# Reading w and u by other DMAs, and a new order for the first unit of an RWKV and SiLU kernel

## Chip, cores and metric

The kernel runs on one core of a Trainium2 chip. The metric is device time in microseconds (us), the median of several executions. A profile shows one execution: its span goes from the first to the last instruction, and the execution's own time is a little longer than its span.

## What is computed

A recurrent attention (RWKV-5 style) over 4 batches, 8 heads, 768 steps and head size 48, followed by a two-layer network with SiLU between its layers:

```python
# r, k, v: (4, 8, 768, 48); w, u: (8, 48)
for t in range(S):
    kt, vt, rt = k[:, :, t], v[:, :, t], r[:, :, t]
    cur = einsum('bhd,bhe->bhde', u[None] * kt, vt)
    y[:, :, t] = einsum('bhd,bhde->bhe', rt, state + cur)
    state = w[None, :, :, None] * state + einsum('bhd,bhe->bhde', kt, vt)
x = y.transpose(0, 2, 1, 3).reshape(B * S, H * D)      # (3072, 384)
h = x @ w_in                                           # w_in (384, 2048)
out = (h * sigmoid(h)) @ w_out                         # w_out (2048, 384)
```

## The kernel before

Time is cut into 6 chunks of 128 steps. A unit is one chunk of one batch; the 24 units run chunk by chunk, batch by batch, so units 0 to 3 are the first chunk of the four batches. Inside a unit the recurrence becomes matrix work: r is multiplied by powers of w, k by inverse powers of w (both with the head dimension on the partitions, two heads to a pair and four pairs to a unit), their product is masked to the strict lower triangle (`am`), and the masked scores times v give y. The term with u on the diagonal is a sum of r*k*u over the head dimension (`rku`), times v (`vu`), added to y.

All is issued by hand in one fixed order (`manual_schedule`); each engine takes its instructions in that order, and waits between engines follow from what tiles they share. Several queues matter here.

- SP issues the loads: r, k and v of a unit are three DMAs of 192 KB (`load`, L71), in 192-byte rows. The loads of units 0 to 3 go out at once; those of units 4 and 5 are held back by a small GpSimd memset (L464) that overlaps one of their destinations.
- VectorE makes the powers of w (`pif`, seven doubling products, L156), the decay products (`p1`, L226 for r, L230 for k), the masks (`am`, L276), the bonus sums (L197) and y (L300).
- GpSimd (POOL) makes k*u (`ku`, L180), r*k*u (`rku_f`, L186), v times the bonus (`vu`, L203), and k scaled for the state (`kc`, L191). It also asks for moe_w_in, which its DMAs turn into half precision on the way, in four parts of 512 columns (`win_part`, L417). Ahead of the first stands a one-column copy of r of unit 1 into `gate` (L434), so that it isn't asked for before that load has landed.
- TensorE transposes r and k, multiplies, and runs the first layer (`l1`, L358: one column tile of 128 is three matmuls) and the second (`l2`, L370) as fillers between the units' work. Junk matmuls (`spin`, L125) keep it busy at the start.

At the very start w and u are each read as four short rows (`wrow`, `urow`, L85: one DMA of 1.5 KB each). A TensorE transpose turns w into columns in PSUM (`to_cols`, L129), from which VectorE starts the powers. Five spins stand ahead of that transpose and four behind it. u goes through a transpose, an ACT copy (L134), four transposes of a broadcast column (`to_rows`, L147) and an ACT copy (L149) to become `u_bc`, u spread over all 128 partitions. This is called between the r and the k product of unit 0 (`mid`).

The order around unit 0 on GpSimd: gate, first part of moe_w_in, ku and rku_f of unit 0, ku and rku_f of unit 1, second part of moe_w_in, vu of unit 1, ku and rku_f of unit 2, kc of unit 0, third and fourth part, the memset at L464.

Of the kernel before, what the change touches and what calls it, by code (L numbers as in the profile page):

```python
# [8 lines left out]
FP = mybir.dt.float32  # L9
F16 = mybir.dt.float16  # L10
AF = mybir.ActivationFunctionType
ALU = mybir.AluOpType
# [3 lines left out]
def kernel(  # L16
# [11 lines left out]
    nc = tc.nc  # L28

    B, H, S, D = r.shape  # L30
    C = 128
    NCH = S // C
    HD = H * D
    NP = H // 2
    PW = 2 * D
    PR = 64 + D
# [7 lines left out]
    cst = ctx.enter_context(tc.tile_pool(name="cst", bufs=1))  # L44
    big = ctx.enter_context(tc.tile_pool(name="big", bufs=1))
    wrk = ctx.enter_context(tc.tile_pool(name="wrk", bufs=2))
    ps = ctx.enter_context(tc.tile_pool(name="ps", bufs=1, space=bass.MemoryType.PSUM))
# [3 lines left out]
    rin = [big.tile([128, H, 64], FP, name=f"rin{i}") for i in range(NIN)]  # L51
# [9 lines left out]
    def unit(i):  # L61
        return divmod(i, B)

    def load(i, mid=None):
        if i >= NU:
            return
        sc, b = unit(i)
        for t, src in ((rin, r), (kin, k), (vin, v)):
            if t is vin and mid:
                mid()  # L70
            nc.sync.dma_start(out=t[i % NIN][:, :, 0:D],  # L71
                              in_=src[b, :, sc * C:sc * C + C, :]
                              .rearrange("h t d -> t h d"))

    wrow = cst.tile([NP, 2, 64], FP)
    urow = cst.tile([NP, 2, 64], FP)
    junk = cst.tile([128, 512], F16)
    nc.vector.memset(junk, 0.0)  # L80
    for t in (wrow, urow):
        nc.vector.memset(t[:, :, D:64], 1.0)

    def load_row(t, src):
        nc.sync.dma_start(out=t[:, :, 0:D], in_=bass.AP(tensor=src.tensor, offset=0,  # L85
                                                        ap=[[PW, NP], [D, 2], [1, D]]))

    load_row(wrow, w)
    load(0, mid=lambda: load_row(urow, u))
    for i in range(1, B):  # L90
        load(i)
    for t in (rin, kin):
        nc.vector.memset(t[0][:, :, D:64], 0.0)
    ident = cst.tile([128, 128], FP)
# [5 lines left out]
        out=maskM, in_=maskM, compare_op=ALU.is_ge, fill=0.0,  # L100
# [17 lines left out]
    def spin(n, t=None):  # L118

        if t is None:  # L120
            t = ps.tile([128, 512], FP, name="spin", tag="t", bufs=5)
        else:
            t = t.rearrange("s p t -> s (p t)")
        for _ in range(n):
            nc.tensor.matmul(t, junk[:, 0:128], junk, start=True, stop=True)  # L125

    def to_cols(row, copy):
        t = ps.tile([128, 512], FP, name="cols", tag="t", bufs=5)
        nc.tensor.transpose(t[0:PR, 0:NP], row.rearrange("p j d -> p (j d)")[:, 0:PR],  # L129
                            ident[0:NP, 0:NP])  # L130
        if copy is None:
            return t[0:PR, 0:NP]
        c = cst.tile([PR, NP], FP, name="cols_sb")
        copy(out=c, in_=t[0:PR, 0:NP])  # L134
        return c

    spin(5)
    wT = to_cols(wrow, None)
    spin(4)
    u_bc = cst.tile([128, H, D], FP)  # L140
    lamC = cst.tile([128, H, D], FP)

    def to_rows(dst, cols):

        t = ps.tile([128, NP, 2, 64], FP, name="rows", tag="t", bufs=5)
        for p in range(NP):
            nc.tensor.transpose(t[:, p, :, :].rearrange("t j d -> t (j d)")[:, 0:PR],  # L147
                                cols(p), ident[0:PR, 0:PR])
        nc.scalar.copy(out=dst.rearrange("t (p j) d -> t p j d", j=2), in_=t[:, :, :, 0:D])  # L149


    nc.vector.tensor_copy(out=pi[:, 0:NP, 1:2], in_=wT.unsqueeze(2))
    nc.vector.reciprocal(out=pi[:, NP:2 * NP, 1:2], in_=wT.unsqueeze(2))
    n = 1
    while n < C:
        nc.vector.tensor_tensor(  # L156
            out=pi[:, :, 1 + n:1 + 2 * n], in0=pi[:, :, 1:1 + n],
            in1=pi[:, :, n:n + 1].broadcast_to([PR, 2 * NP, n]), op=ALU.mult)
        n *= 2
    lamR = pi[:, 0:NP, 0:C]  # L160
    lamK = pi[:, NP:2 * NP, 1:C + 1]
# [15 lines left out]
    def nat_ku(i):  # L177
        L = live.setdefault(i, {})
        L["ku"] = wrk.tile([128, H, D], FP, name="ku")
        nc.gpsimd.tensor_tensor(out=L["ku"], in0=kin[i % NIN][:, :, 0:D], in1=u_bc,  # L180
                                op=ALU.mult)

    def nat_rk(i):
        L = live[i]
        L["rku_f"] = wrk.tile([128, H, D], FP, name="rku_f")
        nc.gpsimd.tensor_tensor(out=L["rku_f"], in0=rin[i % NIN][:, :, 0:D], in1=L["ku"],  # L186
                                op=ALU.mult)
# [12 lines left out]
    def bonus_vu(i):  # L200
        L = live[i]
        L["vu"] = wrk.tile([128, H, D], FP, name="vu", bufs=3)
        nc.gpsimd.tensor_tensor(out=L["vu"], in0=vin[i % NIN],  # L203
                                in1=L["rku"].unsqueeze(2).broadcast_to([128, H, D]),
                                op=ALU.mult)
# [5 lines left out]
            nc.scalar.activation(out=L["vu"][:, h, :], in_=vin[i % NIN][:, h, :],  # L211
                                 func=AF.Copy, scale=L["rku"][:, h:h + 1])

    def p1(i, mid=None, spins=0):
        n = i % NIN
        L = live.setdefault(i, {})
        tr = ps.tile([128, NP, C], FP, name="tr", tag="t", bufs=5)
        tk = ps.tile([128, NP, C], FP, name="tk", tag="t", bufs=5)
        spin(spins, tr)
        for t, src in ((tr, rin), (tk, kin)):  # L220
            flat = src[n].rearrange("p h d -> p (h d)")
            for p in range(NP):
                nc.tensor.transpose(t[0:PR, p, :], flat[:, 128 * p:128 * p + PR], ident)  # L223
        rk = wrk.tile([PR, 2, NP, C], FP, name="rk")
        L["rT"] = rk[:, 0]
        nc.vector.tensor_tensor(out=L["rT"], in0=tr[0:PR], in1=lamR, op=ALU.mult)  # L226
        if mid:
            mid()
        L["kT"] = rk[:, 1]
        nc.vector.tensor_tensor(out=L["kT"], in0=tk[0:PR], in1=lamK, op=ALU.mult)  # L230

    def p1t(i):

        n = i % NIN
        L = live.setdefault(i, {})
        xs = [ps.tile([128, 2, NP, 64], FP, name="xs", tag="t", bufs=5) for _ in range(2)]
        for a, src in enumerate((rin, kin)):
            flat = src[n].rearrange("p h d -> p (h d)")
            for p in range(NP):
                for g in range(2):  # L240
                    t = slice(64 * g, 64 * g + 64)
                    nc.tensor.transpose(xs[g][0:PR, a, p, :],  # L242
                                        flat[t, 128 * p:128 * p + PR], ident[t, t])
        rk = wrk.tile([PR, 2, NP, C], FP, name="rk")
        L["rT"] = rk[:, 0]
        L["kT"] = rk[:, 1]
        L["xs"] = xs, rk
# [13 lines left out]
    def p2(i, spins=0, nxt=None, late=False):  # L261
        L = live[i]
        ae = ps.tile([128, NP, C], FP, name="ae", tag="t", bufs=5)
        ao = ps.tile([128, NP, C], FP, name="ao", tag="t", bufs=5)
        spin(spins, ae)
        for p in range(NP):
            nc.tensor.matmul(ae[:, p, :], L["kT"][0:D, p, :], L["rT"][0:D, p, :],  # L267
                             start=True, stop=True)
            nc.tensor.matmul(ao[:, p, :], L["kT"][64:PR, p, :], L["rT"][64:PR, p, :],  # L269
                             start=True, stop=True)  # L270
        if nxt is not None:
            p1t(nxt)
        L["am"] = []
        for a in (ae, ao):
            am = wrk.tile([128, NP, C], F16, name="am", bufs=4)
            nc.vector.tensor_tensor(out=am, in0=a,  # L276
                                    in1=maskM.unsqueeze(1).broadcast_to([128, NP, C]),
                                    op=ALU.mult)
            L["am"].append(am)
        if nxt is not None and not late:  # L280
            p1d(nxt)
# [124 lines left out]
            f()  # L406


    def to_cols_u():
        t = to_cols(urow, nc.scalar.copy)  # L410
        to_rows(u_bc, lambda p: t[:, p:p + 1].broadcast_to([PR, 128]))

    zero = junk[0:PR, 0:HD].rearrange("r (p c) -> r p c", p=NP)
    gate = cst.tile([128, 1], FP)

    def win_part(c0, c1):
        nc.gpsimd.dma_start(out=win[:, :, c0:c1],  # L417
                            in_=moe_w_in[:, c0:c1].rearrange("(q p) n -> p q n", p=128))
# [4 lines left out]
            in_=moe_w_out[1024 * g:1024 * g + 1024, :].rearrange("(f p) n -> p f n", p=128))  # L423


    p1(0, mid=to_cols_u)
    nat_v(0)
    lamCT = cst.tile([PR, NP, C], FP)
    for p in range(NP):
# [1 line left out]
                             scale=pi[:, p, C:C + 1])  # L431

    nc.scalar.copy(out=st[0], in_=zero)
    nc.gpsimd.tensor_copy(out=gate, in_=rin[1][:, 0, 0:1])  # L434
    win_part(0, 512)
    nat_ku(0)
    nat_rk(0)
    p2(0)
    p1(1, spins=1)
    bonus_sum(0)  # L440
    nat_ku(1)
# [3 lines left out]
    to_rows(lamC, lambda p: lamCT[:, p, :])  # L445
    bonus_act(0)
    nc.scalar.copy(out=st[1], in_=zero)
    win_part(512, 1024)
    bonus_sum(1)
    bonus_vu(1)  # L450
    p2(1, spins=2)
    p3e(0)
    spin(4)
# [2 lines left out]
    spin(1)  # L456
    p4(0)
    p1(2)
    nat_ku(2)
    nat_rk(2)  # L460
# [177 lines left out]
```

## Time and profile before

| what | value |
|---|---|
| median of 11 runs | 198.71 us (198.15 to 199.88) |
| the profiled execution's own time | 199.09 us |
| its span | 197.4 us |
| TensorE matmul busy | 189.8 us, 96% of the span |
| VectorE, ScalarE, GpSimd busy | 115.4, 91.1, 115.0 us |
| granted TensorE clock, of full speed | 0.999 |
| DMA, mean rate | 122 GB/s over the span; 167 to 209 GB/s from 5 to 55 us |
| one load of 192 KB, issue to landing | 3.5 to 3.8 us in the median |
| a part of moe_w_in, issue to landing | 6.1 us in the median |

How to read it: DVE is VectorE, ACT is ScalarE, POOL is GpSimd, PE is TensorE's matmuls and PEld its weight loads, which run ahead of and beside the matmuls. A row of the timeline gives the start, the duration, the engine, the source line, the operation with its output and inputs, and in brackets the idle time of the engine before it with what ended that. The share of busy time is a mean over the whole; TensorE's first 16 us are partly spins, and after some 25 us it is hardly ever idle.

### The profile page before, as it was taken

What the parts mean: (1) busy time and instruction counts of PE and PEld (TensorE: products, weight loads), DVE (VectorE), ACT (ScalarE), POOL (GpSimd) and SP (SyncE); (2) the same over time, 40 slices, a digit from 0 to 9 for tenths busy, and PEclk for the clock granted to TensorE, in tenths of its full rate; (3) what the DMA queues carried; (4) which work ended last, traced back from release to release, by engine and by line L of the source; (5) the groups of instructions that cost most, each with busy time, mean ns of one, the idle gap of its engine ahead of it and who ended that gap; (6) DMA issues with size and microseconds to landing.
All of it is one profiled execution on the core that took longest, in us unless ns stands there. A gap on an engine that the chain in (4) does not pass through costs nothing.

```text
span 197.4 us, 4920 instructions
## 1 busy us (share of the span) xinstructions
PE 189.8 (96%) x1919; PEld 127.4 (65%) x1919; DVE 115.4 (58%) x233; ACT 91.1 (46%) x207; POOL 115.0 (58%) x145
## 2 busy tenths in 40 slices
PE   7889999999999999999999999999999999999993
PEld 2747878787765976675566766557666546644563
DVE  6677658885857746975675686476576344210121
ACT  3475487799212652205861216682016680069300
POOL 4499959979975795697669647735437710000000
PEclk9999999999999999999999999999999999999999
DMA  4999999999898976757466387520321011210022
GB/s 82 209 186 167 186 203 179 184 189 202 165 196 176 221 173 149 173 136 160 89 122 140 100 182 160 105 58 0 106 60 43 20 22 43 78 61 0 3 81 80
DMA packets 89696, 24.12 MB, mean 122 GB/s; under 512 B 82888, under 2 KB 89672, under 8 KB 89672
## 3 DMA queue, kind: packets, MB, share of 16 engines
q1 hardware_dynamic: 85992, 20.66, 48.1%
q0 software_dynamic: 3680, 3.15, 10.9%
q8 instruction: 15, 0.25, 0.5%
q14 instruction: 9, 0.07, 0.1%
HBM read 20.45 MB, written 4.72 MB: 128 GB/s over the span
## 4 chain that ended last, share of the span: by engine, by line
PE 86%; DVE 5%; POOL 2%; ACT 2%; issue 2%; DMA 1%; DVEq 0%; POOLq 0%
PE hps L358 30%; PE ops L370 29%; PE ae L267 11%; PE xs L242 4%; PE y L293 3%; DVE am L276 2%; PE spin L125 2%; PE y L290 2%; PE sps L309 1%; PE ops L384 1%; DMA xT<-y 1%; POOL rku_f L186 1%; POOL ku L180 1%; PE tr L223 1%; PE tk L223 1%
## 5 line engine op out<-in xcount | busy, mean ns | idle before, releaser
L361 ACT ACTIVATE gT<-hps 128x256 f16<-128x256 f32 (+1 forms) x128 | 59.7, 493 | 47.3 <-PE hps L358 45.6
L358 PE MATMUL hps<-xT,win 128*128 128x256 f16 (+1 forms) x384 | 69.2, 326 | 0.9 <-DMA xT<-y 0.4
L370 PE MATMUL ops<-wout,gT 128*128 128x384 f16 x368 | 63.8, 326 | 0.0
L358 PEld LDWEIGHTS <-win 128*128 128x128 f16 x384 | 35.5, 98 | 23.9 <-issue 1.9
L370 PEld LDWEIGHTS <-gT 128*128 128x128 f16 x368 | 34.6, 98 | 22.4
L276 DVE TENSOR_TENSOR am<-ae,maskM 128x512 f16<-128x512 f32 x24 | 16.6, 691 | 36.0 <-PE ao L269 35.9
L374 DVE COPY osb<-ops 128x384 f32<-128x384 f32 x23 | 12.7, 553 | 27.3 <-PE ops L370 27.2
L259 ACT CAST rT<-rk 112x512 f16<-112x512 f32 x20 | 12.3, 615 | 35.2 <-DVE rk L253 35.2
L267 PEld LDWEIGHTS ae<-rk 48*128 48x128 f32 x192 | 23.1, 187 | 7.7 <-issue 4.2
L267 PE MATMUL ae<-rk 48*128 48x128 f32 x192 | 27.7, 285 | 0.3 <-DVE rk L230 0.3
L269 PE MATMUL ao<-rk 48*128 48x128 f32 x192 | 27.7, 285 | 0.0
L203 POOL TENSOR_TENSOR vu<-vin,rku 128x384 f32<-128x384 f32 x23 | 19.1, 829 | 12.9 <-DVE rku L197 12.8
L253 DVE TENSOR_TENSOR rk<-xs,pif 112x512 f32<-112x512 f32 x40 | 25.5, 680 | 1.7 <-PE xs L242 1.7
L180 POOL TENSOR_TENSOR ku<-kin,u_bc 128x384 f32<-128x384 f32 x24 | 24.1, 1005 | 2.2 <-DMA kin<-in_k_dram 2.1
L186 POOL TENSOR_TENSOR rku_f<-rin,ku 128x384 f32<-128x384 f32 x24 | 24.1, 1005 | 1.9
L191 POOL TENSOR_TENSOR kc<-kin,lamC 128x384 f16<-128x384 f32 x24 | 24.0, 1001 | 0.0
L269 PEld LDWEIGHTS ao<-rk 48*128 48x128 f32 x192 | 23.1, 187 | 0.0
L323 POOL CAST stb<-st 112x384 f16<-112x384 f32 x12 | 6.0, 502 | 22.8 <-DVE st L318 22.8
L300 DVE TENSOR_TENSOR y<-y,vu 128x384 f16<-128x384 f32 x24 | 13.4, 556 | 7.6 <-POOL kc L191 2.3
L276 DVE TENSOR_TENSOR am<-ao,maskM 128x512 f16<-128x512 f32 x24 | 16.3, 680 | 0.0
L197 DVE TENSOR_REDUCE rku<-rku_f 128x8 f32<-128x384 f32 x24 | 13.2, 549 | 2.3 <-POOL rku_f L186 1.8
L325 POOL TENSOR_TENSOR sdec<-st,pif 112x384 f32<-112x384 f32 x16 | 13.3, 835 | 1.1 <-ACT gT L361 1.1
(74 smaller groups left out, 169.6 us busy)
## 6 DMA issues: line engine op xcount, KB each, us to landing
rin<-in_r_dram SPq DMA_DIRECT2D x24, 192.0 KB, 3.5
kin<-in_k_dram SPq DMA_DIRECT2D x24, 192.0 KB, 3.8
vin<-in_v_dram SPq DMA_DIRECT2D x24, 192.0 KB, 3.6
out_dram<-osb SPq DMA_DIRECT2D x23, 192.0 KB, 1.9
win<-in_moe_w_in_dram POOLq DMA_DIRECT2D x4, 384.0 KB, 6.1
wout<-in_moe_w_out_dram POOLq DMA_DIRECT2D x2, 768.0 KB, 11.0
xT<-y SPq DMA_TRANSPOSE x18, 2.3
out_dram<-osh SPq DMA_DIRECT2D x1, 128.0 KB
```

The costliest lines, as they stand in the source:

```text
L180: nc.gpsimd.tensor_tensor(out=L["ku"], in0=kin[i % NIN][:, :, 0:D], in1=u_bc, op=ALU.mult)
L186: nc.gpsimd.tensor_tensor(out=L["rku_f"], in0=rin[i % NIN][:, :, 0:D], in1=L["ku"], op=ALU.mult)
L191: nc.gpsimd.tensor_tensor(out=kc[i % NKC][:, :, 0:D], in0=kin[n][:, :, 0:D], in1=lamC, op=ALU.mult)
L203: nc.gpsimd.tensor_tensor(out=L["vu"], in0=vin[i % NIN], in1=L["rku"].unsqueeze(2).broadcast_to([128, H, D]), op=ALU.mult)
L253: nc.vector.tensor_tensor(out=rk[:, :, :, 64 * g:64 * g + 64], in0=xs[g][0:PR], in1=lam(g), op=ALU.mult)
L267: nc.tensor.matmul(ae[:, p, :], L["kT"][0:D, p, :], L["rT"][0:D, p, :], start=True, stop=True)
L269: nc.tensor.matmul(ao[:, p, :], L["kT"][64:PR, p, :], L["rT"][64:PR, p, :], start=True, stop=True)
L276: nc.vector.tensor_tensor(out=am, in0=a, in1=maskM.unsqueeze(1).broadcast_to([128, NP, C]), op=ALU.mult)
L300: nc.vector.tensor_tensor(out=L["y16"], in0=L["y"], in1=L["vu"], op=ALU.add)
L358: nc.tensor.matmul(hps, win[:, q, ft * 128:(ft + 1) * 128], xts[sc][:, q, b0:b1, :].rearrange("p b t -> p (b t)"), start=(q == 0), stop=(q ...
L361: nc.scalar.activation(out=gts[sc][:, ft, b0 * C:b1 * C], in_=hps, func=AF.Silu)
L370: nc.tensor.matmul(ops, gts[sc][:, ft, b * C:(b + 1) * C], wout[:, ft, :], start=(ft == 0), stop=(ft == NFT - 1))
```

## The change

- w is read straight into columns, `wcol` (112 partitions by 4), by two DMAs, one issued by SP (rows 0 to 47) and one by ACT (rows 64 to 111). Rows 32 to 63 are set to one before, by a VectorE memset.
- u is read by one DMA that repeats its 384 values over 128 partitions straight into `u_bc`. It stands where u's short DMA stood, between k and v of unit 0.
- The transposes and copies that made columns and rows of w and u go, with `to_cols`; ten spins stand in one row.
- For unit 0 alone the two decay products are made in halves of two pairs each, in the order r, k, r, k.
- In the order of GpSimd, ku of unit 0 comes ahead of the gate and the first part of moe_w_in; rku_f of unit 0 follows them. The score matmuls of unit 0 (`p2(0)`) are written ahead of ACT's copy of v and its four scaled copies. The second part of moe_w_in moves behind vu of unit 1.

```diff
-    wrow = cst.tile([NP, 2, 64], FP)
-    urow = cst.tile([NP, 2, 64], FP)
+    wcol = cst.tile([PR, NP], FP)
+    u_bc = cst.tile([128, H, D], FP)
     junk = cst.tile([128, 512], F16)
     nc.vector.memset(junk, 0.0)
-    for t in (wrow, urow):
-        nc.vector.memset(t[:, :, D:64], 1.0)
...
-    load_row(wrow, w)
-    load(0, mid=lambda: load_row(urow, u))
+    nc.vector.memset(wcol[32:64, :], 1.0)
+    for j, e in ((0, nc.sync), (1, nc.scalar)):
+        e.dma_start(out=wcol[64 * j:64 * j + D, :],
+                    in_=bass.AP(tensor=w.tensor, offset=D * j, ap=[[1, D], [PW, NP]]))
+
+    def load_u():
+        nc.sync.dma_start(out=u_bc.rearrange("t h d -> t (h d)"),
+                          in_=bass.AP(tensor=u.tensor, offset=0, ap=[[0, 128], [1, HD]]))
+
+    load(0, mid=load_u)
...
-    spin(5)
-    wT = to_cols(wrow, None)
-    spin(4)
-    u_bc = cst.tile([128, H, D], FP)
+    spin(10)
...
+    wT = wcol
     nc.vector.tensor_copy(out=pi[:, 0:NP, 1:2], in_=wT.unsqueeze(2))
...
-        nc.vector.tensor_tensor(out=L["rT"], in0=tr[0:PR], in1=lamR, op=ALU.mult)
-        if mid:
-            mid()
         L["kT"] = rk[:, 1]
-        nc.vector.tensor_tensor(out=L["kT"], in0=tk[0:PR], in1=lamK, op=ALU.mult)
+        step = NP // 2 if i == 0 else NP
+        for q in range(0, NP, step):
+            q = slice(q, q + step)
+            for x, t, lam_ in (("rT", tr, lamR), ("kT", tk, lamK)):
+                nc.vector.tensor_tensor(out=L[x][:, q], in0=t[0:PR, q], in1=lam_[:, q],
+                                        op=ALU.mult)
...
-    p1(0, mid=to_cols_u)
+    p1(0)
+    nat_ku(0)
+    nc.gpsimd.tensor_copy(out=gate, in_=rin[1][:, 0, 0:1])
+    win_part(0, 512)
+    nat_rk(0)
+    p2(0)
     nat_v(0)
...
     nc.scalar.copy(out=st[0], in_=zero)
-    nc.gpsimd.tensor_copy(out=gate, in_=rin[1][:, 0, 0:1])
-    win_part(0, 512)
-    nat_ku(0)
-    nat_rk(0)
-    p2(0)
     p1(1, spins=1)
...
     nc.scalar.copy(out=st[1], in_=zero)
-    win_part(512, 1024)
     bonus_sum(1)
     bonus_vu(1)
+    win_part(512, 1024)
     p2(1, spins=2)
```

More of the change, by code (lines that the diff above doesn't have):

```diff
@@ L73, in load @@
                               .rearrange("h t d -> t h d"))
-    wrow = cst.tile([NP, 2, 64], FP)
-    urow = cst.tile([NP, 2, 64], FP)
+    wcol = cst.tile([PR, NP], FP)
+    u_bc = cst.tile([128, H, D], FP)
     junk = cst.tile([128, 512], F16)
     nc.vector.memset(junk, 0.0)
-    for t in (wrow, urow):
-        nc.vector.memset(t[:, :, D:64], 1.0)
-    def load_row(t, src):
-        nc.sync.dma_start(out=t[:, :, 0:D], in_=bass.AP(tensor=src.tensor, offset=0,
-                                                        ap=[[PW, NP], [D, 2], [1, D]]))
-    load_row(wrow, w)
-    load(0, mid=lambda: load_row(urow, u))
+    nc.vector.memset(wcol[32:64, :], 1.0)
[6 more added lines that the diff above has]
+    load(0, mid=load_u)
     for i in range(1, B):
@@ L125, in spin @@
             nc.tensor.matmul(t, junk[:, 0:128], junk, start=True, stop=True)
[L127 to L135, printed above, removed]
-    spin(5)
-    wT = to_cols(wrow, None)
-    spin(4)
-    u_bc = cst.tile([128, H, D], FP)
+    spin(10)
     lamC = cst.tile([128, H, D], FP)
@@ L212, in bonus_act, with p1 @@
                                  func=AF.Copy, scale=L["rku"][:, h:h + 1])
-    def p1(i, mid=None, spins=0):
+    def p1(i, spins=0):
         n = i % NIN
@@ L406, in fill @@
             f()
-    def to_cols_u():
-        t = to_cols(urow, nc.scalar.copy)
-        to_rows(u_bc, lambda p: t[:, p:p + 1].broadcast_to([PR, 128]))
     zero = junk[0:PR, 0:HD].rearrange("r (p c) -> r p c", p=NP)
```

## The prediction

> **What bounds the kernel now.** I read the page first (TensorE busy for 96% of the span, the chain of waits 86% on it), so a change in the first 20 us counts only if it moves the point from which TensorE is never short of work again. I therefore read the timeline from 0 to 28 us engine by engine, the waits of that stretch, and the landing times of single DMAs, each asked for in a window around its issue.
>
> VectorE, the first 15 us (start, duration, engine, line, what; idle before it in brackets):
> ```profile
> 3.79 0.17 DVE L152 COPY pif<-cols 112x4 f32<-112x4 f32 x1 [0.83 <-PE cols L129]
> ...
> 6.60 0.69 DVE L226 TENSOR_TENSOR rk<-tr,pif 112x512 f32<-112x512 f32 x1
> 7.21 0.68 DVE L230 TENSOR_TENSOR rk<-tk,pif 112x512 f32<-112x512 f32 x1
> 9.13 0.69 DVE L276 TENSOR_TENSOR am<-ae,maskM 128x512 f16<-128x512 f32 x1 [1.25 <-PE ao L269]
> ...
> 11.54 0.54 DVE L197 TENSOR_REDUCE rku<-rku_f 128x8 f32<-128x384 f32 x1
> 13.09 0.55 DVE L197 TENSOR_REDUCE rku<-rku_f 128x8 f32<-128x384 f32 x1 [1.01 <-POOL rku_f L186]
> 13.56 0.68 DVE L276 TENSOR_TENSOR am<-ae,maskM 128x512 f16<-128x512 f32 x1
> ```
> The reader is to see two things. Unit 0 hangs on VectorE from the columns of w (3.79) to the second decay product (7.21). But unit 1's masking (13.56) stands behind the bonus sum at 13.09, and that one waited 1.01 us for GpSimd.
>
> GpSimd from 7.8 us:
> ```profile
> 7.83 0.19 POOL L434 COPY gate<-rin 128x1 f32<-128x1 f32 x1 [5.10 <-DMA rin<-in_r_dram]
> 7.95 0.93 POOL L417 DMA_DIRECT2D win<-in_moe_w_in_dram  x1
> 8.90 1.03 POOL L180 TENSOR_TENSOR ku<-kin,u_bc 128x384 f32<-128x384 f32 x1
> 10.01 1.00 POOL L186 TENSOR_TENSOR rku_f<-rin,ku 128x384 f32<-128x384 f32 x1
> ...
> 12.99 0.80 POOL L417 DMA_DIRECT2D win<-in_moe_w_in_dram  x1
> 13.82 0.84 POOL L203 TENSOR_TENSOR vu<-vin,rku 128x384 f32<-128x384 f32 x1
> 14.64 1.00 POOL L180 TENSOR_TENSOR ku<-kin,u_bc 128x384 f32<-128x384 f32 x1
> ...
> 17.63 1.57 POOL L417 DMA_DIRECT2D win<-in_moe_w_in_dram  x2
> 19.19 0.12 POOL L464 MEMSET rin<- 128x1 f32 x1
> ```
> It begins when unit 1's r has landed (7.83) and then does not pause until 20 us: this stretch dates the four requests for moe_w_in.
>
> TensorE's weight loads that consume the quarters, and the landing of the last two:
> ```profile
> 24.02 1.21 PEld L358 LDWEIGHTS <-win 128*128 128x128 f16 x12
> 25.23 0.47 PEld L293 LDWEIGHTS <-am 128*128 128x128 f16 x8
> 25.63 0.58 PEld L358 LDWEIGHTS <-win 128*128 128x128 f16 x6
> ```
> ```profile
> L417 POOL DMA_DIRECT2D win<-in_moe_w_in_dram x2: 772/787/802, 17.6 to 18.4; - x2
> ...
> DMA to landing us min/median/max: 5.7/6.4/7.1
> ```
> Three weight loads make one column tile of moe_w_in. Counted from the first at 16.79, the x12 at 24.02 are tiles 8 to 11 (third quarter) and the x6 at 25.63 tiles 12 and 13 (fourth). The third quarter lands at 17.63 + 5.7 = 23.3, the fourth at 18.4 + 7.1 = 25.5. So the fourth has about 0.1 us to spare and the third 0.7: this is the place where the head is really measured.
>
> **What the Trainium skill says.** "DMA: Bandwidth & Descriptors", section "Issuing engines are not separate DMA queues": DMAs started from several engines share the same 16 DMA engines; only issue time is saved. The trace agrees that the engines are the limit: from 4 to 9 us 5370 packets of 192 bytes took 103.6% of 16 engines. Same page, "Queues, rings and completion order": an engine takes turns between queue rows, packet by packet. Here the turns are very uneven: from 11 to 12 us GpSimd's queue moved 174 packets and SP's 47; once a quarter of moe_w_in flows, the loads nearly stop. Same page, "Rules for kernel authors": a non-contiguous last dimension gives one descriptor per element; no run here shows 4-byte rows yet.
>
> **The change part by part.**
>
> w as columns. It removes a TensorE transpose (3.50, done at 3.75) between w's landing and VectorE. But the memset of rows 32 to 64 overlaps the rows 0 to 47 that SP's half writes, so SP's first DMA must wait for it. VectorE clears junk at 0.93 and its next memset ran 1.15 to 1.24, so SP starts near 1.3 instead of 0.80. Each half is 192 four-byte elements, 12 per engine; at the 15 ns that a 192-byte packet took (16 x 5 us / 5370) that is 0.2 us, and it may be several times that. DMA activity shows the old w moving 1.5 to 1.8 us after its issue. I take 3.5 for VectorE's start against 3.79 (bounds 3.1 and 4.5). ACT's half issues beside it, ahead of ACT's table load; ACT was idle to 6.87.
>
> Halves. A 512-column product takes 0.69 and follows the last after 0.61; 384 columns take 0.56, so 256 take about 0.43, one per 0.35. Four halves are 1.4 us against 1.3, but the first eight score matmuls go after two of them. The chain from the columns to the first product is 6.60 - 3.79 = 2.8, so products run 6.3 to 7.8 and the last eight matmuls (half of the 1.16 us that sixteen took) end near 8.6 instead of 9.1. The k halves also need k of unit 0, which lands at about 2.17 + 3.6 = 5.8 now and 0.4 later then: no stall beyond that. Unit 0's masking comes 0.45 earlier, unit 1's products about 0.4 (bounds 0 and 0.7).
>
> Spins and u's rows. Ten spins at 0.43 from 1.26 end at 5.5, as five, the transpose and four did (5.36). u's TensorE and ACT pieces (0.2, 0.6, 0.16, 0.48) go; they lay beside VectorE's products and are worth nothing by themselves.
>
> u by broadcast. The write is 192 KB instead of 1.5 KB, put between k and v of unit 0: 128 packets of 1536 bytes, 8 per engine. The 1536-byte reads of moe_w_out between 38.2 and 39.8 went at 16 x 1.6 / 313 = 82 ns each: 0.65 us (bounds 0.5, and 1.0 as for an ordinary load). SP's late start adds 0.4 (0.2 to 0.5). All loads behind it are late by s = 0.65 + 0.4, about 1.05 us (0.7 to 1.5), since the engines are full from 3 us.
>
> GpSimd's order. unit 0's ku, 1.1 us in the sequence, moves ahead of the gate into idle time; u lands near 7.0 there, well before the gate. The gate goes to 7.83 + 1.05 = 8.9. So rku of unit 1 ends at 13.05 + 1.05 - 1.11 = 13.0: no change, and the VectorE gain of 0.4 ends in a longer wait for it. Then the second quarter, whose 0.80 of issue filled GpSimd's wait for the bonus sum, comes behind vu: vu starts at 13.6 instead of 13.8, and the issue stands alone from 14.5 to 15.3. ku of unit 2 comes at 15.3 by GpSimd alone, but k of unit 2 landed at 7.69 + 6.9 = 14.6 behind the first quarter, and both shift by s: 15.6. Queued behind it are rku, kc, the third and fourth quarter, and the memset that releases SP's loads of unit 4. All come 0.65 to 1.0 later.
>
> Sum: the fourth quarter lands at 26.2 to 26.5 instead of 25.5. TensorE, whose masks for units 1 to 3 come as before, needs it at 25.63 and stalls. Less the 0.1 to spare this is 0.6 to 0.9; I take 0.8. The loads of unit 4 (k landed 26.9, with GpSimd waiting on it) shift by as much, so nothing is regained: behind it TensorE is full. Span 197.4 + 0.8; the profiled execution took 199.09, 1.7 more than its span, so it would be 199.9. The median of the runs shown is 0.4 below it: 199.5.
>
> **The rivals.**
>
> A slow broadcast or slow element DMAs: 128 reads of one row, or 4-byte writes at several times 15 ns, push s to 1.8 or w to 5. For it: neither form is in the trace. Against: packets of every size there keep their pace. Time 198.7 + 1.7 = 200.4.
>
> GpSimd gains (the case on the other side): ku leaves the stretch behind the gate, and that stretch sets both unit 1's mask and the later quarters. By GpSimd alone the requests move by s + 0.7 (the issue that stands alone) - 1.1, so s = 0.4 is the point from which it decides: below it, if SP is not held and the broadcast fits into the slack of the first DMAs, the quarters come early. At s = 0 they come 0.4 earlier and unit 1's mask up to 0.8, which is 0.4 to 0.8 faster, the upper end if TensorE has more room before tiles 12 and 13 than I count: 198.0. For it: GpSimd's unbroken stretch. Against: full DMA engines from 3 us.
>
> No effect: both cancel within 0.6, 198.7, if k of unit 2 escapes the first quarter and s stays at 0.7.
>
> **How the numbers follow.** Forecast 0.55 (own range 199.2 to 200.0), slow DMAs 0.10, GpSimd gains 0.24, no effect 0.11. About 0.3%, 0.6 us, is what can be told from no change. Nearly all of the first two lies above it, and most of the third below. The range 197.8 to 200.4 takes in both signs.
>
> **What would show it.** VectorE's first copy near 3.5 and unit 0's mask near 8.7; the gate near 8.9; the bonus sum of unit 1 still near 13; the third quarter asked for near 18.5; a new idle of TensorE before tiles 12 and 13 near 25.6. A gate before 8.2, or no idle there, proves me wrong.

## The result and the profile after

The changed kernel takes 201.2 us (median of 12 runs; the kernel before, measured beside it, 198.64). Three of the 12, at 203.3 to 205.4 us and a mean granted clock of 0.992, are slow executions and are left out of the ratio. The ratio is 1.0112, with a 95% interval of 1.009 to 1.0133: 2.2 us slower. The forecast, 199.5 us, had the sign and the chain and was too small; 201.2 lies outside its range. The profiled execution took 201.19 us, its span 199.5, against 199.09 and 197.4.

The chain of waits of the changed kernel, from its start (start, duration, what):

```profile
1.80 0.43 SPq L71
2.27 0.58 SPq L71
2.89 5.02 DMA u_bc<-in_u_dram
8.06 1.00 POOL ku L169
9.06 0.38 issue
9.46 0.19 POOL gate L415
```

Before, the chain ran over TensorE's spins and transposes here. Now it lies for 5.02 us on one DMA, u's broadcast. GpSimd in the same stretch:

```profile
8.06 1.00 POOL L169 TENSOR_TENSOR ku<-kin,u_bc 128x384 f32<-128x384 f32 x1 [5.32 <-DMA u_bc<-in_u_dram]
9.46 0.19 POOL L415 COPY gate<-rin 128x1 f32<-128x1 f32 x1 [0.40 <-DMA rin<-in_r_dram]
...
15.04 0.80 POOL L404 DMA_DIRECT2D win<-in_moe_w_in_dram  x1
16.53 1.00 POOL L169 TENSOR_TENSOR ku<-kin,u_bc 128x384 f32<-128x384 f32 x1 [0.69 <-DMA kin<-in_k_dram]
...
19.50 1.57 POOL L404 DMA_DIRECT2D win<-in_moe_w_in_dram  x2
```

The gate comes at 9.46 instead of 7.83: the loads behind u are 1.6 us late. ku of unit 2 waits for its k, as forecast (16.53, before 14.64), and the third and fourth quarter of moe_w_in are asked for 1.87 us late. VectorE:

```profile
3.31 0.17 DVE L141 COPY pif<-wcol 112x4 f32<-112x4 f32 x1 [0.19 <-DMA wcol<-in_w_dram]
...
6.66 0.42 DVE L220 TENSOR_TENSOR rk<-tr,pif 112x256 f32<-112x256 f32 x1 [0.68 <-PE tr L212]
...
9.09 0.69 DVE L267 TENSOR_TENSOR am<-ae,maskM 128x512 f16<-128x512 f32 x1 [0.80 <-PE ao L260]
...
13.64 0.55 DVE L186 TENSOR_REDUCE rku<-rku_f 128x8 f32<-128x384 f32 x1 [1.49 <-POOL rku_f L175]
14.11 0.68 DVE L267 TENSOR_TENSOR am<-ae,maskM 128x512 f16<-128x512 f32 x1
```

The columns of w do start the powers 0.48 us earlier (3.31, before 3.79). In this execution the gain is lost at the next step, where the first product now waits 0.68 us for TensorE's transposes of r. Unit 0's mask begins at 9.09 against 9.13. Unit 1's bonus sum waits for GpSimd longer than before, so unit 1's mask begins at 14.11 instead of 13.56; unit 2's begins at 19.49 instead of 18.92, and unit 3's at 25.01 instead of 24.12.

TensorE's weight loads at the quarters, and then its matmuls at the end of the second chunk:

```profile
24.98 1.21 PEld L349 LDWEIGHTS <-win 128*128 128x128 f16 x12 [0.20 <-DMA win<-in_moe_w_in_dram]
...
27.18 0.55 PEld L349 LDWEIGHTS <-win 128*128 128x128 f16 x6 [0.57 <-DMA win<-in_moe_w_in_dram]
```

```profile
61.91 2.11 PE L361 MATMUL ops<-wout,gT 128*128 128x384 f16 x12
65.33 0.81 PE L349 MATMUL hps<-xT,win 128*128 128x256 f16 x6 [1.31 <-DMA xT<-y]
```

The new idle before column tiles 12 and 13 is the one that was forecast. It is only 0.57 us long because TensorE comes there about 0.9 us late already (unit 3 in the table below); the landing of the fourth quarter is the wait that ends last.

The wait of 1.31 us at 65 us was not forecast. There TensorE needs y of unit 7, turned by a DMA transpose that stands in SP's queue behind loads. In the changed kernel VectorE has this y ready at 55.2 us, and the transpose is asked for at 62.63:

```profile
54.61 0.56 DVE L291 TENSOR_TENSOR y<-y,vu 128x384 f16<-128x384 f32 x1
62.63 1.20 SPq L331 DMA_TRANSPOSE xT<-y  x1
```

In the kernel before, it is asked for 1.90 us earlier, and the same wait is 0.45 us:

```profile
60.73 1.20 SPq L340 DMA_TRANSPOSE xT<-y  x1
63.18 0.81 PE L358 MATMUL hps<-xT,win 128*128 128x256 f16 x6 [0.45 <-DMA xT<-y]
```

The start of each unit's score matmuls (of their first weight load) shows how the loss builds up:

| unit | before, us | after, us | difference |
|---|---|---|---|
| 0 | 7.94 | 7.68 | -0.26 |
| 1 | 11.67 | 11.95 | +0.28 |
| 2 | 17.72 | 18.30 | +0.58 |
| 3 | 22.92 | 23.82 | +0.90 |
| 4 | 30.30 | 31.59 | +1.29 |
| 8 | 56.55 | 57.85 | +1.30 |
| 9 | 63.92 | 66.07 | +2.15 |
| 23 | 162.85 | 164.99 | +2.14 |

So there are two steps: 1.3 in the head (the first units, up to where TensorE is full), reached by unit 4, and 0.85 at unit 9. Both are read from one execution of each kernel.

### The profile page after: what moved, and what is told of

Read it like the earlier page. It is cut to its first block, busy times and chain, and to the rows that moved or that the text cites. A ratio compares the mean times of both kernels' runs of the same rounds, so it can differ in the third digit from the quotient of the medians.

```text
span 199.5 us, 4908 instructions
## 1 busy us (share of the span) xinstructions
PE 190.0 (95%) x1914; PEld 127.4 (64%) x1914; DVE 116.0 (58%) x234; ACT 90.7 (45%) x205; POOL 115.1 (58%) x145
## 4 chain that ended last, share of the span: by engine, by line
PE 81%; DVE 6%; DMA 4%; POOL 3%; ACT 2%; issue 2%; SPq 1%; DVEq 0%; POOLq 0%
PE ops L361 29%; PE hps L349 28%; PE ae L258 11%; PE xs L233 4%; DMA u_bc<-in_u_dram 3%; PE y L284 2%; DVE am L267 2%; PE y L281 2%; PE sps L300 1%; PE ops L375 1%; DMA xT<-y 1%; ACT gT L352 1%; POOL rku_f L175 1%; POOL ku L169 1%; DVE y L291 1%
## 5 line engine op out<-in xcount | busy, mean ns | idle before, releaser
L164 ACT CAST v<-vin 128x384 f16<-128x384 f32 x24 | 12.2, 507 | 8.2 <-DMA vin<-in_v_dram 8.2
```

## The experiments

Theory "broadcast": reading u's one row 128 times holds up the DMA engines, the loads behind it, and with them the head. Rival "order": the new places of ku and of the second quarter on GpSimd cost the time. A third theory, on the wait at unit 9, came from the table above. The ratios are to the kernel before, measured on the same chip, with 95% intervals.

### u by a short row again, all else as changed

```diff
-    load(0, mid=load_u)
+    nc.scalar.dma_start(out=urow[:, :, 0:D], in_=bass.AP(tensor=u.tensor, offset=0, ...))
+    load(0)
...
-    spin(10)
+    spin(5)
+    ucol = to_cols(urow, nc.scalar.copy)
+    spin(1)
...
+    to_rows(u_bc, lambda p: ucol[:, p:p + 1].broadcast_to([PR, 128]))
+    spin(1)
```

> The changed kernel, but u comes as one short row DMA (1.5 KB, asked for by ACT behind its half of w) and is turned and spread by TensorE and ACT between seven spins; SP then has only r, k and v behind its half of w. Theory 'broadcast' (the 128 reads of u's one row slow the DMA engines, so every load behind comes 1.6 us late, and that is most of the loss): the gate falls to 7.9 to 8.3 us from 9.46, the last quarter of moe_w_in lands by 25.9, and the time is 198.5 to 199.3. Theory 'order' (ku ahead of the gate and the second quarter behind vu are the loss): the time stays at 200.2 or more.

198.48 us, ratio 0.9987 (0.9956 to 1.0018). GpSimd:

```profile
5.97 1.00 POOL L184 TENSOR_TENSOR ku<-kin,u_bc 128x384 f32<-128x384 f32 x1 [3.24 <-DMA kin<-in_k_dram]
7.36 0.19 POOL L430 COPY gate<-rin 128x1 f32<-128x1 f32 x1 [0.39 <-DMA rin<-in_r_dram]
```

The gate is even earlier than expected, 7.36, and the loss is gone with the broadcast. "Order" falls as its cause: both of its moves are still in this kernel. Everything else in the change, w's columns, the halves and the order, together with the move of u's row to ACT's queue, comes to no measurable difference.

### The broadcast alone, in the kernel before

```diff
-    load(0, mid=lambda: load_row(urow, u))
+    load(0, mid=load_u)
...
-    p1(0, mid=to_cols_u)
+    p1(0)
```

> The kernel before with u read by the broadcast DMA in place of its short row, and nothing else changed. Theory 'broadcast': the gate comes at 8.9 to 9.2 instead of 7.83, the time is 199.9 to 200.8. Theory 'order': within 0.6 of before, 198.1 to 199.2.

201.62 us, ratio 1.013 (1.0089 to 1.0171; four runs): more than expected, and again on the side of "broadcast". The gate, too, is later than expected, at 9.56. Here a second effect joins, seen in the stages of this kernel's profile (the stretch and its length; busy us and, in parentheses, instructions of PE, PEld, DVE, ACT and POOL; then the granted TensorE clock, the DMA share and GB/s):

```profile
14.00:16.00 2.00, 0.12 (x1) 0.00 (x0) 1.19 (x3) 1.67 (x7) 1.98 (x3) 1.00 1.22 221
16.00:18.00 2.00, 1.58 (x14) 1.27 (x15) 1.58 (x3) 0.13 (x1) 1.40 (x3) 0.64 1.13 175
18.00:20.00 2.00, 2.00 (x12) 1.74 (x11) 1.12 (x2) 0.45 (x2) 2.00 (x3) 0.51 1.22 221
```

While unit 1 waits for its bonus sum, TensorE has nothing to do from 14.1 to 16.0 us, and then it works at half clock from 16.5 to about 20 us. Its unit 2 begins 3.1 us later than before, unit 1 only 0.3. Of the 3.1, 1.7 are there when the y matmuls of unit 1 begin (16.02, before 14.30); the other 1.4 come in the stretch at half clock. Three of the four runs had a low mean clock (0.991, 201.3 to 202.0 us); the fourth, at full clock, took 200.36, 1.7 above before. So the ratio holds two effects, and the size of the broadcast's own rests on one run.

### The same transfer from other rows

```diff
-                          in_=bass.AP(tensor=u.tensor, offset=0, ap=[[0, 128], [1, HD]]))
+                          in_=bass.AP(tensor=moe_w_out.tensor, offset=0, ap=[[HD, 128], [1, HD]]))
```

> The changed kernel with the broadcast's source replaced by 128 different rows of 1536 bytes (the first 128 of moe_w_out), so u's values are replaced; size, packets, place and queue are the same. Theory 'one row' (reading one row 128 times is what is slow): the transfer lands 1.0 us or more earlier, the gate at 8.5 to 8.9, time 199.3 to 200.2, which is what the forecast assumed. Theory 'any large write there' (192 KB at that place cost it whatever the source): gate within 0.2 of 9.46, time 200.7 to 201.5.

199.29 us, ratio 1.0017 (0.9994 to 1.004). The DMA view from 5 to 8 us (40 slices of 75 ns: tenths busy, and GB/s) of the changed kernel, and of this one:

```profile
DMA  9457222332222265757966858788778999999999
GB/s 200 146 136 118 85 77 67 72 67 56 49 51 64 74 200 156 184 164 195 197 123 195 197 154 115 172 167 159 164 146 189 197 177 215 223 223 230 213 202 210
```

```profile
DMA  9997999999999999998899999999999999999999
GB/s 282 443 356 289 310 343 277 266 253 274 251 256 274 251 254 261 243 192 179 164 202 205 184 205 241 228 215 205 213 210 238 228 236 256 256 228 220 230 233 169
```

```profile
8.00 0.19 POOL L415 COPY gate<-rin 128x1 f32<-128x1 f32 x1 [0.69 <-DMA rin<-in_r_dram]
```

With 128 different rows the engines stay full. With one row they are two to three tenths busy from 5.3 to 6.05 us, at 49 to 85 GB/s: they wait rather than work, and for what is not shown. k of unit 0 landed at 2.27 + 3.2 = 5.5 in the changed kernel and u at 2.9 + 5.0 = 7.9, which is 2.4 us; here it is 5.6 and 2.9 + 3.3 = 6.2, 0.6 us. With the one row the other loads went on meanwhile (1517 of the 1626 packets of these 3 us are under 512 bytes), so u's 2.4 us came to 1.63 at the gate. With 128 rows the gate is at 8.00, only 0.17 later than before. That the size of the write matters ("any large write there") falls.

The same with eight neighbouring rows, each read 16 times:

```diff
+                          in_=bass.AP(tensor=moe_w_out.tensor, offset=0, ap=[[0, 16], [HD, 8], [1, HD]]))
```

> The changed kernel with the broadcast's source replaced by eight neighbouring rows of 1536 bytes (of moe_w_out), each read 16 times[...]; u's values are replaced. If only reading a single row 128 times is slow: as with 128 different rows, landing by 6.4 us and gate near 8.0. If any repeated reading of few rows is slow: landing at 7.3 or later, gate 8.8 or later.

```profile
6.90 1.00 POOL L169 TENSOR_TENSOR ku<-kin,u_bc 128x384 f32<-128x384 f32 x1 [4.17 <-DMA u_bc<-in_moe_w_out_dram]
8.11 0.19 POOL L415 COPY gate<-rin 128x1 f32<-128x1 f32 x1 [0.22 <-DMA rin<-in_r_dram]
```

It landed at 2.9 + 3.9 = 6.8, a little later than expected, the gate is at 8.11, and the time 199.21 us, ratio 1.0017 (0.9991 to 1.0043). Eight rows are nearly as good as 128, so sixteen readings of each row cost little. Both of these runs read moe_w_out, though, and one row of moe_w_out read 128 times was not tried. That the repeating of one row is slow, and not the place in memory where u lies, is therefore the likely reading and not shown.

### The second quarter ahead of vu again

```diff
+    win_part(512, 1024)
     bonus_sum(1)
     bonus_vu(1)
-    win_part(512, 1024)
```

> The changed kernel with the second quarter of moe_w_in asked for ahead of vu of unit 1 again, as before. Theory 'broadcast': no gain, since ku of unit 2 waits for k of unit 2 (landed at 16.45) and not for GpSimd: within 0.5 of the changed kernel, 200.5 to 201.5. Theory 'order': at least 0.7 faster, 200.3 or less.

200.37 us, ratio 1.008 (1.0056 to 1.0104), just between the two expectations, and the interval overlaps the changed kernel's. In its profile ku of unit 2 still waits for its k, at 16.38 instead of 16.53, and unit 4 is 1.13 us late instead of 1.29; the rest of the difference stands at unit 9, where the wait for y of unit 7 was 0.6 us instead of 1.31. A gain from this move, 0.6 us by the two ratios, can't be excluded, nor shown.

### The wait at unit 9

y of units 6 and 7 is turned by TensorE and ACT, as y of units 0 to 5 is:

```diff
-        if i >= NIN:
+        if i >= 2 * B:
             nc.sync.dma_start_transpose(out=xts[sc][:, :, b, :],
```

In the changed kernel, and in the kernel before:

> The changed kernel with y of units 6 and 7 turned by TensorE and copied by ACT, as units 0 to 5 are, instead of by a DMA transpose; nothing else. In the profile of the changed kernel TensorE was 1.30 us late from unit 4 to unit 8 and 2.15 us from unit 9 on, and there it waited 1.31 us for the DMA transpose of unit 7. Theory 'load queue' (the loads run 1.7 to 2.1 us late in SP's queue, and the transpose stands behind them): the lateness stays near 1.3 to 1.5 to the end and the time is 0.5 us or more below the changed kernel, 199.9 to 200.7. Theory 'chance' (the wait is the spread of single executions): within 0.4 of the changed kernel, 200.8 to 201.6.

> The same edit in the kernel before, where TensorE waited only 0.45 us at that place. Theory 'load queue': within 0.4 us of before, 198.2 to 199.0, so that the gain in the changed kernel isn't the edit's own. Otherwise, if the edit is simply better: 0.6 or more below before, 198.0 or less.

The changed kernel so edited takes 200.68 us, ratio 1.0116 (1.0091 to 1.014); the kernel before, 199.49 us, ratio 1.0054 (1.0033 to 1.0075). By its ratio the first is no faster than the changed kernel (1.0112); its time lies where "load queue" put it, but the gain of 0.5 us did not come. The second misses what was expected of it: the edit costs 1.1 us of its own. So the pair has to be read against each other: 1.2 us apart, where the unedited kernels are 2.2 apart, with about half a microsecond of uncertainty on each. In the profiles unit 9 and all later units are 1.91 and 0.41 us late, 1.5 apart, which is the lateness at unit 4 in these two profiles (1.49 and 0.00). With the DMA transposes of units 6 and 7 gone the head's loss alone remains between the two. That supports "load queue", by which the head's 1.3 us and a wait of nearly 1 us in SP's queue make up the 2.2, but does not prove it. The next runs have such a wait too.

### What the loads' dates are worth

Five variants start the loads earlier or take up the gain elsewhere.

```diff
# both halves of w by ACT, in the variant with u's short row
-    for j, e in ((0, nc.sync), (1, nc.scalar)):
-        e.dma_start(
+    for j in (1, 0):
+        nc.scalar.dma_start(
...
# the kernel before: short rows by ACT
-        nc.sync.dma_start(out=t[:, :, 0:D], in_=bass.AP(tensor=src.tensor, offset=0,
+        nc.scalar.dma_start(out=t[:, :, 0:D], in_=bass.AP(tensor=src.tensor, offset=0,
```

> The variant with u's short row (e1_u_short_row), with both halves of w asked for by ACT as well, so that SP starts with r of unit 0 at 0.8 us instead of 1.8. Theory 'the dates of the loads set the head': the gate falls from 7.36 to 6.4 to 6.7, all that follows comes 0.5 to 1.0 us earlier, time 197.3 to 198.1. Theory 'the VectorE chain sets the head': gate earlier, time within 0.3 of that variant, 198.2 to 198.8.

> The kernel before with one word changed: the short rows of w and u are asked for by ACT instead of SP, so that SP starts with r of unit 0 at 0.8 us instead of 1.7, and u's 0.65 us of issue goes from between k and v. Theory 'dates of the loads': gate at 6.7 to 7.1 instead of 7.83, time 197.5 to 198.2. Theory 'the VectorE chain': w's columns come when they came, time within 0.3 of before.

The first was a failure of its own making: 200.08 us, ratio 1.0073 (1.0055 to 1.009). u's row, third in ACT's queue, came so late that TensorE waited for it (one spin more stands ahead of it here), with the transposes of r and k behind, and that ku stood in front of the gate and held it:

```profile
5.13 0.22 PE L131 MATMUL cols<-ident,urow 4*112 4x4 f32 x1 [1.13 <-DMA urow<-in_u_dram]
...
7.24 1.00 POOL L184 TENSOR_TENSOR ku<-kin,u_bc 128x384 f32<-128x384 f32 x1 [4.50 <-ACT u_bc L150]
8.18 0.19 POOL L430 COPY gate<-rin 128x1 f32<-128x1 f32 x1
```

Unit 0's mask came at 10.50, where the variant it was made from had 8.51. So it tells nothing of the loads' dates, but it shows the danger in the change's order: ku ahead of the gate is free only while u is early. The second, 198.14 us, ratio 0.9993 (0.9975 to 1.0011), has the gate at 6.23 and still no measurable gain: ku waits for ACT's copy of u, at 8.21, so 1.6 us on the loads become 0.6 at unit 2. This fits both expectations.

The last two steps move the third quarter ahead of kc of unit 0, in the variant with u's short row and in the kernel before with short rows by ACT:

```diff
-    nat_kc(0)
     win_part(1024, 1536)
+    nat_kc(0)
     win_part(1536, 2048)
```

> The variant with u's short row (e1_u_short_row), with the third quarter of moe_w_in asked for ahead of kc of unit 0 instead of behind it, 1.0 us earlier on GpSimd. In that variant's profile TensorE still waited 0.7 us in all for moe_w_in, although it was 0.9 us early before that. Theory 'the quarters eat the gain': these waits go and the time falls by 0.3 to 0.8 to 197.7 to 198.2. Theory 'something else behind it binds' (the loads of units 3 and 4, which the earlier quarter pushes back): no gain, 198.3 to 199.

> The same edit in the variant of the kernel before whose short rows are asked for by ACT (e8_before_act_rows). There TensorE waited for no quarter, so the theory 'the quarters eat the gain' expects no change: 198.0 to 198.4.

198.18 us, ratio 0.9985 (0.9963 to 1.0007), and 198.05 us, ratio 0.9976 (0.9961 to 0.9991). Both times lie where they were expected, but the first interval includes no change, and its profile speaks against the theory. In the variant without this move TensorE waited 0.37 us for the fourth quarter (the 0.7 above counts the wait of the weight loads and that of the matmuls behind them, which are one). Now that wait is gone, TensorE waits for y of unit 3 instead, and unit 4 begins only 0.05 us earlier:

```profile
26.02 0.34 PE L352 MATMUL yT<-ident,y 128*128 128x128 f16 x3 [0.32 <-DVE y L306]
```

The second is the only version measured below both kernels, by 0.24%.

> The variant with u's short row and the earlier third quarter, with SP starting on r of unit 0 at 0.8 us (SP's half of w stands behind that r), and the gate and the first quarter ahead of ku of unit 0 as before. Theory 'dates of the loads': gate 6.3 to 6.7, VectorE's first copy 3.6 to 4.0 (0.3 to 0.7 later than with w ahead), time 197.3 to 198.0. Theory 'VectorE and GpSimd set the head by now': 198.0 to 198.6.

This one also puts SP's half of w behind r of unit 0 (`load(0, mid=...)` before k) and the gate ahead of ku. 198.55 us, ratio 1.0 (0.9981 to 1.0019), with the gate at 6.84: no gain, the second expectation. Its runs go from 197.9 to 200.7 us, and the profiled one was the slowest. TensorE's waits from 12 to 75 us there (engine, line, waited for: us in total, times, longest):

```profile
PE hps L366 <- DMA xT<-y: 1.6, 1, 1.6
```

It is the wait at unit 9 again, in a kernel without the broadcast and with early loads. The profiled run of the variant with u's short row and the earlier third quarter, 200.33 us and its slowest, has one of 1.3 us as well. So that wait is not the broadcast's own. Late loads may make it likelier, as the pair above suggests; one trace of each kernel can't show how often it comes, and how much of the changed kernel's 0.85 us it adds in a typical run stays open.

## Why the prediction was right in kind and wrong in size

**The failing step** is "u by broadcast": 128 packets at 82 ns over 16 engines, 0.65 us with bounds 0.5 and 1.0. It took 2.4 us. So s, the lateness of the loads behind it, was 1.63 at the gate and not 1.05. With 128 different rows all of s, transfer and late start together, was 0.17; the other 1.46 go with reading u's one row. The rate came from the reads of moe_w_out, which are of different rows, and for different rows it holds: 0.6 us was measured. The bounds took the size of a packet for its whole price; where it is read from was not in them. The rival "a slow broadcast", with 1.7 us, named this mechanism as "128 reads of one row" and got 0.10; its s of 1.8 was nearly right, and the evidence against it, packets "of every size", was evidence about something else. That the one row is slow because it is one row, and not because of where it lies, stays open.

**SP's late start**, 0.4 us, was too dear. SP does wait for the memset and starts at 1.34, but its half of w took 0.40 us to issue where the short row took 0.84, so r of unit 0 was asked for at 1.80 instead of 1.71. With the broadcast's rows replaced the gate came only 0.17 late.

**w's columns** came at 3.31 (forecast 3.5), and the four-byte elements were no trouble. The forecast 0.45 us at unit 0's mask became 0.04 in the profiled run: TensorE's transposes, ready 0.35 us ahead of need before, were the next thing to be late, and I had not asked what follows once the powers are early. This date is not the change's alone. In the two runs with other rows, which are the changed kernel up to there, the same ten spins took 3.65 and 3.70 us instead of 4.45, and the mask came at 8.34 and 8.67, near the 8.7 of the forecast; why the spins differ is not shown. In the variant with u's short row the mask came at 8.51. That unit 1's bonus sum swallows the gain was right.

**GpSimd's chain** was right link by link from the gate to the fourth quarter: ku ahead of the gate in idle time, the second quarter alone behind vu, ku of unit 2 held by its k, the third and fourth quarter late by s and more, the memset too, and TensorE idle before tiles 12 and 13. With s = 1.6 instead of 1.05 the fourth quarter landed at 20.3 + 6.8 = 27.1 (forecast 26.2 to 26.5), and the head lost 1.3 instead of 0.8. The masks of units 1 to 3, which were to come as before, came 0.55, 0.57 and 0.89 late. That follows from the same s: with 1.63 in place of 1.05, the forecast's sum for rku of unit 1 gives 13.57 and not 13.0, and its bonus sum began at 13.64.

**"Behind it TensorE is full"** was wrong in one place. Loads and DMA transposes share SP's queue; with the loads late, the transpose of unit 7 was asked for 1.90 us late, and 0.85 us were added there in the profiled run. The profile before showed the place: a wait of 0.45 us, so no slack at all. That the late loads are the cause is supported by the pair of runs above and not proved.

**GpSimd gains**, the case on the other side, had a point: below s = 0.4 it should win. At s = 0.17 and 0.28 (the two runs with other rows) the ratio was 1.0017; by this rival's own sum the quarters come only 0.2 and 0.1 us earlier there, less than can be told. Where the gate was early (7.36) it was 0.9987, no measurable gain: a head start of 0.9 us at unit 3 shrank to 0.5 at unit 4, and that rest does not show in the runs.

## What to carry to other kernels

Price a DMA by what it reads as well as by its packets: here a small operand repeated over the partitions out of one memory row took 2.4 us, four times what the same transfer took from 128 rows, and the loads queued behind it paid. A short row turned and spread on idle engines was the cheaper way here. And after working out a delay, follow it to every queue that it shifts, not only to the engine that sets the end: each wait in the profile before, however small, is a place where a late queue can add its own share.

## What the runs showed of the hardware

- One row of 1536 bytes read 128 times: 2.4 us from the landing before it to its own, at 49 to 85 GB/s in its slow part, 0.75 us long. Eight rows 16 times each: landed at 6.8 us, against 6.2 for 128 rows and 7.9 for one. The one row was u's, the others moe_w_out's.
- TensorE idle for 1.9 us (14.1 to 16.0) was followed by half clock from 16.5 to some 20 us. The Trainium skill, "TensorE: Matmul & The Clock Gate", section "Part 1: The HAM clock gate", gives an idle window of about 3.4 us for this; here less was enough, and the half clock cost some 1.4 us on top of the wait.
- Two DMAs of 192 four-byte elements, asked for at 0.81 and 1.34 us, were there for VectorE at 3.31. The way by a short row and TensorE's transpose had VectorE start at 3.79.
